# Cosine attention and a leaky-ReLU MLP on one core: where epsilon comes from, where transposes, scalings and key tiles stand in the order

## The chip, the cores and the metric

One core of one Trainium2 chip runs the whole program. The metric is the device time of one execution in microseconds. Five engines work side by side, each with its own instruction queue in program order: TensorE (PE, matrix multiplications; its weight loads are shown as PEld), VectorE (DVE), ScalarE (ACT), GpSimd (POOL) and SyncE (SP, which here only issues DMAs). They meet through semaphores.

## The reference

For 8 batches of 12 heads, 448 positions and 64 dimensions, `q` and `k` are divided by their norms plus an epsilon, and attention is taken with temperature `tau = 0.1`; its output, 3584 rows of 768, goes through a two-layer network with 2048 hidden units.

```python
q_n = q / (np.linalg.norm(q, axis=-1, keepdims=True) + 1e-06)
k_n = k / (np.linalg.norm(k, axis=-1, keepdims=True) + 1e-06)
scores = np.matmul(q_n, k_n.transpose(0, 1, 3, 2)) / tau
attn = np.exp(scores - np.max(scores, axis=-1, keepdims=True))
attn = attn / (np.sum(attn, axis=-1, keepdims=True) + 1e-09)
x = np.matmul(attn, v)            # then laid out as (3584, 768)
h = x @ w_in
out = np.maximum(0.01 * h, h) @ w_out
```

The scores of unit vectors are bounded, so the kernel subtracts no maximum.

## The kernel before

**Slots.** The 48 pairs of heads are 48 slots. For each slot the raw `q` and `k` are loaded (`load_qk`, on SP's queue, into 4 buffers), squared on POOL (`squares`, line 208 for slots 0 to 11, line 201 from slot 12 on), summed on DVE (`sums`, lines 222 and 216), turned into norms on ACT by a logarithm and an exponential (`roots`, lines 229 and 230), and divided on DVE (`normalise`: line 238 adds the epsilon, 239 takes the reciprocal, 255 or 245 multiplies and rounds to bf16, into `qn`). `hold` is a one-element POOL copy of `qn` (line 583): POOL's queue waits there until DVE has finished the multiplication, and the next squares stand behind it. `qn` is then transposed: for slots 0 to 11 by seven PE matmuls (line 269) and a DVE copy out of PSUM (line 310); for later slots by a DVE transpose (line 291), and for every second one of them by six SP DMAs (line 300) that gather two slots, a *unit*, into `qkT`.

**Scores, sums, values.** PE multiplies a tile of keys by all queries (line 331, or 402 in the third stage), ACT takes the exponential out of PSUM (lines 340 and 408). Row sums and values are further PE products of these tiles (line 351, or 427), the sums inverted on ACT by logarithm and exponential (362 and 363, or 436 and 439), and DVE multiplies the value products by them into `xT` (`scale`, line 382; `group_scale`, lines 452 and 458).

**The network.** `first` is one of 16 groups of hidden units for one chunk of columns (line 476, leaky ReLU on ACT at 485), `second` half of the output columns for 128 rows (line 507, DVE copy at 518, output DMA at 527). These groups have no hurry, and stand between pieces of attention.

**PSUM.** The 8 banks are dealt by `banks`, which takes the bank or pair of banks that was dealt longest ago. PE must wait where the work that last used a bank has not been read out of it.

**Stages.** All order is written by hand, with no scheduler behind it.

1. The loop over `s` from 0 to 5 (line 618) does the attention of batch 0, with filler matmuls (line 574) between. `j` counts pairs of slots whose values follow; `totals(j)` are their row sums, `products(j, e)` their values for even (`e = 0`) and odd dimensions, `scale(j, e)` the division. In an even `s` from 2 on, `totals(j)`, `products(j, 0)` and the transposes of slot `s + 1` follow each other on PE. `products(j, 1)` stands in the next, odd `s`, with both scalings: `scale(j, 0)` after its `normalise`, `scale(j, 1)` at its end.
2. A transition (lines 681 to 737), in which slots 6 to 10 are prepared between groups of the network of batch 0, and the key tiles of slots 6 and 7 in blocks.
3. `opened` (line 743), five steps for the rest of batch 1.
4. 42 *visits* (line 822). Each takes three key tiles of 32-column strips (`quad_tiles`), in `preps` visits prepares a slot, in `parts` visits makes the sums (`e = None`) or one half of the values (`e = 0`, `1`) of a group of heads, and is filled up with network groups by a planner that counts their columns. In a visit with a preparation, `normalise(s)` stands first, then `prepare` (transposes, load, `hold`, squares, and the sums of slot `s + 1`, in this order), then the first key tile, and behind it the group's products and scaling. Only where a group has a single member, does `prepare` stand behind the scaling (`alone`). `roots(s + 1)` stands near the visit's end, in front of its last network group, and so ahead of the next visit's exponentials in ACT's queue.
5. What is left of the network.

Of the kernel before, what the change touches and what calls it, by code (L numbers as in the profile page):

```python
# [8 lines left out]
F32 = mybir.dt.float32  # L9
BF16 = mybir.dt.bfloat16  # L10
AF = mybir.ActivationFunctionType
ALU = mybir.AluOpType
# [4 lines left out]
def kernel(  # L17
# [10 lines left out]
    nc = tc.nc  # L28
# [205 lines left out]
    def normalise(s):  # L234
        if s >= NSLOT:
            return
        r = smp.tile([128, 14], F32, name="r")
        nc.vector.tensor_scalar_add(ss[s], ss[s], 1e-6)  # L238
        nc.vector.reciprocal(r, ss[s])  # L239
        if s >= OLD:  # L240


            qn[s] = qnp.tile([128, 7, D, 2], BF16, name="qn")
            t, n = ("(m e)", "(e m)")[s % 2], 2
            nc.vector.tensor_tensor(  # L245
                qn[s].rearrange("p m d e -> p m e d"),
                raw[s].rearrange(f"p ({t[1:-1]} d) -> p m e d", e=n, d=D),
                r.rearrange(f"p {t} -> p m e", e=n).unsqueeze(3).to_broadcast([128, 7, 2, D]),
                op=ALU.mult,
            )  # L250
            return
        qn[s] = qnp.tile([128, 7, 2, D], BF16, name="qn")
        for x, lo, hi, r0 in ((raw[s][0], 0, 4, 0), (raw[s][1], 4, 7, 8)):
            nt = hi - lo
            nc.vector.tensor_tensor(
                qn[s][:, lo:hi],
                x.rearrange("p h t d -> p t h d"),
                r[:, r0 : r0 + 2 * nt].rearrange("p (h t) -> p t h", h=2)
                .unsqueeze(3).to_broadcast([128, nt, 2, D]),
                op=ALU.mult,  # L260
            )
# [55 lines left out]
    def scores(s, kis):  # L317
        key_tiles([(s, ki) for ki in kis])
# [49 lines left out]
    def products(j, e, po=None):  # L368
        b, jj = divmod(j, NQ)
        if po is None:  # L370
            po = banks(1, (j, e))
        pos[j, e] = po
        vm = vb[j].rearrange("p h t (d e) -> p h t e d", e=2)
        vr = vrb[b % 2].rearrange("p j g (d e) -> p j g e d", e=2)
        strip_products(j, po, lambda g, ki: vm[:, g, ki, e], lambda g: vr[:, jj, g, e])
# [177 lines left out]
    load_qk(3)  # L553
    tiny = cpool.tile([128, 1], F32, name="tiny")
    nc.vector.memset(tiny, 1e-18)
    warm = pep.tile([128, 2 * S], BF16, name="pe")[:, 0:512]
    nc.vector.memset(warm, 1.0)
    ones = cpool.tile([128, 32], BF16, name="ones")
# [56 lines left out]
    roots(1)  # L615


    for s in range(NPAIR):
        j = s // 2 - 1 if s >= 2 else None
        even = s % 2 == 0  # L620
        n = s + 2 if 0 < s < NPAIR - 2 else None
        last = s == NPAIR - 1
        if s == 1:
            roots(2)
        scores(s, (0,))
        if j is not None and not even:
            products(j, 1)
        scores(s, (1,))
        fill(2)
        if n:  # L630
            sums(n, (0,))
        if not last:
            normalise(s + 1)
            load_qk(s + 5)
        if j is not None and not even:
            scale(j, 0)
        if last:
            load_v(s // 2 + 1)
            load_v_rem(1)
            load_w_out(0)  # L640
        else:
            hold(qn[s + 1][:, 6, 0, 0:1])
        squares(s + 3)
        if s == 0:
            sums(2)
            load_v_rem(0, range(2, 4))
        if not even and not last:
            load_v(s // 2 + 1)
        if s != 1 and not last:
            load_w_in(max(s - 1, 0))  # L650
        if n:
            sums(n, (1,))
        scores(s, (2,))
        if not even or s == 0:
            fill(2)
        if n and not even:
            roots(n)
        if not even:
            scores(s, (3,))
        if j is not None and even:  # L660
            totals(j)
            products(j, 0)
        if not last:
            transposes(s + 1)
        if not even or s == 0:
            fill(2)
        if n and even:
            roots(n)
        if j is not None and not even:
            scale(j, 1)  # L670

    def attend(j):
        totals(j)
# [7 lines left out]
    deals["apart"] = False  # L681
    deals["width"] = 64
    s, j = NPAIR, NQ - 1
    totals(j)
    sums(s)
    po = banks(2)
# [19 lines left out]
    normalise(s + 1)  # L706
    load_qk(s + 5)
    sums(s + 2)
    scores(s, (0, 1))
    feed_groups(0, 1)  # L710
    transposes(s + 1)
    roots(s + 2)
    feed_groups(0, 1)
    scores(s, (2,))
    scores(s + 1, (0,))
    normalise(s + 2)
    hold(qn[s + 2][:, 6, 0, 0:1])
    squares(s + 4)
# [1 line left out]
    load_w_out(1)  # L720
    sums(s + 3)
    feed_groups(0, 2)
    transposes(s + 2)
    roots(s + 3)
    scores(s + 1, (1, 2))
    normalise(s + 3)
    load_qk(s + 6)
    sums(s + 4)
    feed_groups(0, 2)
    transposes(s + 3)  # L730
    roots(s + 4)
    scores(s + 1, (3,))
    normalise(s + 4)
    load_qk(s + 7)
    hold(qn[s + 4][:, 6, 0, 0:1])
    squares(s + 5)
    feed_groups(0, 3)

# [81 lines left out]
    for n, tiles in enumerate(visits):  # L822
        s = preps.get(n, NSLOT)
        g, e = parts.get(n, (None, None))
        alone = g is not None and e is not None and len(GROUPS[g]) == 1

        def prepare():
            if s < NSLOT:
# [4 lines left out]
                sums(s + 1)  # L833

        normalise(s)
        if not alone:
            prepare()
        quad_tiles(tiles[:1])
        if n == 0:
# [1 line left out]
        if g is not None:  # L841
# [2 lines left out]
                group_logs(g, po)  # L844
            else:
                group_scale(g, e, po)
        if alone:
            prepare()
        quad_tiles(tiles[1:])
        if g is not None and e is None:  # L850
# [73 lines left out]
```

## Time and profile before

| | us |
|---|---|
| median of 3 runs | 428.2 |
| lowest and highest | 426.79, 428.51 |
| the profiled execution | 426.59 |
| its span | 424.8 |

The span runs from the first to the last instruction that the profiler saw; 1.79 us of the profiled execution lie around it. PE is busy for 411.5 us of the span, ACT for 255.5, DVE for 221.6 and POOL for 114.8. The granted TensorE clock is full speed throughout. A row of the timeline has start, duration, engine, line, operation, tiles and shape; in brackets the time that the engine sat idle before it and what ended that. Several instructions of a kind are merged into one row (x16). "Slot 10" or "unit 1" below are names of this text for what the code counts so.

### The profile page before, as it was taken

The numbers are of one execution on the slowest core, as the hardware profiler recorded it, in microseconds if no ns is written. First come the engines' busy times: TensorE is split into PE (matmuls) and PEld (weight loads), VectorE is DVE, ScalarE is ACT, GpSimd is POOL, SyncE is SP. The second block draws the span as 40 slices with busy tenths as digits, with TensorE's granted clock in tenths as the row PEclk, the third lists the DMA queues.
The fourth block names the chain that finished last, engine by engine and source line by source line (L and its number), as shares of the span: only waits on it lengthen the run. The fifth ranks groups of instructions, "written<-read, shape, count | busy, mean of one in ns | idle before, by whom it ended". The sixth has DMA issues, their size and how long they took to land.

```text
span 424.8 us, 11331 instructions
## 1 busy us (share of the span) xinstructions
PE 411.5 (97%) x4779; PEld 213.6 (50%) x4797; DVE 221.6 (52%) x382; ACT 255.5 (60%) x430; POOL 114.8 (27%) x149
## 2 busy tenths in 40 slices
PE   7889999989999999999999999999999999999996
PEld 3334555434455555554455555554445555554563
DVE  5966877775578554776474874376412312120021
ACT  3886885668857686748875767647674454104300
POOL 3867353533234132413231432023010000000000
PEclk9999999999999999999999999999999999999999
DMA  6899999875375963575375583544441100010021
GB/s 170 163 236 226 215 239 175 195 208 144 56 201 156 214 156 58 158 175 144 78 162 146 116 231 91 115 125 125 83 88 39 77 38 3 36 76 0 2 74 74
DMA packets 41906, 53.82 MB, mean 127 GB/s; under 512 B 12544, under 2 KB 32256, under 8 KB 41856
## 3 DMA queue, kind: packets, MB, share of 16 engines
q1 hardware_dynamic: 25536, 40.85, 34.0%
q0 software_dynamic: 15488, 11.80, 19.4%
q8 instruction: 37, 0.61, 0.6%
q10 hardware_dynamic: 832, 0.46, 0.4%
q14 instruction: 13, 0.11, 0.1%
HBM read 45.61 MB, written 11.01 MB: 133 GB/s over the span
## 4 chain that ended last, share of the span: by engine, by line
PE 82%; DVE 8%; ACT 4%; DMA 3%; issue 2%; SPq 0%; POOL 0%; ACTq 0%; POOLq 0%; DVEq 0%
PE ps L476 32%; PE ps L507 31%; PE ps L427 8%; PE ps L402 6%; DMA qk_h<-in_k_dram 2%; PE ps L351 2%; PE ps L331 2%; DVE ss L216 1%; DVE qn L245 1%; DMA qk_h<-in_q_dram 1%; ACT pe L340 1%; ACT pe L408 1%; PE ps L269 1%; DVE ss L238 1%; DVE xT L382 1%
## 5 line engine op out<-in xcount | busy, mean ns | idle before, releaser
L507 PE MATMUL ps<-w_out_sb,hT 128*128 128x384 bf16 x896 | 151.4, 326 | 0.2 <-DVE xT L382 0.2
L476 PE MATMUL ps<-xT,w_in_sb 128*128 128x384 bf16 (+1 forms) x753 | 149.7, 352 | 0.9 <-issue 0.2
L408 ACT ACTIVATE pe<-ps 128x896 bf16<-128x896 f32 x126 | 109.1, 916 | 47.1 <-PE ps L402 43.2
L507 PEld LDWEIGHTS <-hT 128*128 128x128 bf16 x896 | 85.3, 98 | 64.7 <-issue 10.4
L476 PEld LDWEIGHTS <-w_in_sb 128*128 128x128 bf16 x768 | 73.1, 98 | 73.7 <-issue 8.4
L485 ACT ACTIVATE hT<-ps 128x384 bf16<-128x384 f32 (+1 forms) x128 | 68.0, 548 | 63.0 <-PE ps L476 62.2
L518 DVE COPY osb<-ps 128x384 f32<-128x384 f32 (+1 forms) x56 | 30.8, 550 | 106.4 <-PE ps L507 100.7
L201 POOL TENSOR_TENSOR sq<-qk_h 128x896 f32<-128x896 f32 x36 | 60.5, 1680 | 3.1 <-DMA qk_h<-in_q_dram 2.1
L583 POOL CAST seen<-qn 128x1 f32<-128x1 bf16 x46 | 8.5, 185 | 179.8 <-DVE qn L245 167.3
L245 DVE TENSOR_TENSOR qn<-qk_h,r 128x896 bf16<-128x896 f32 x36 | 42.7, 1185 | 1.4 <-DVE r L239 0.2
L402 PE MATMUL ps<-qkT 64*32 64x448 bf16 x1008 | 39.1, 353 | 2.0 <-DVE xT L382 1.4
L340 ACT ACTIVATE pe<-ps 128x896 bf16<-128x896 f32 x42 | 36.0, 916 | 7.4 <-PE ps L331 7.3
L216 DVE TENSOR_REDUCE ss<-sq 128x14 f32<-128x896 f32 x36 | 37.5, 1041 | 2.6 <-POOL sq L201 2.6
L238 DVE TENSOR_SCALAR ss<-ss 128x14 f32<-128x14 f32 x48 | 11.0, 230 | 49.1 <-ACT ss L230 48.8
L291 DVE STREAM_TRANSPOSE tt<-qn 128x448 f32<-128x448 f32 x36 | 29.6, 824 | 1.2
L452 DVE TENSOR_TENSOR xT<-ps,rb 128x448 bf16<-128x448 f32 x32 | 18.3, 613 | 21.5 <-PE ps L427 21.4
L427 PE MATMUL ps<-pe,vq 64*32 64x448 bf16 x1008 | 27.3, 349 | 0.0
L402 PEld LDWEIGHTS <-qkT 64*32 64x32 bf16 x1008 | 14.2, 91 | 23.2 <-issue 18.6
L229 ACT ACTIVATE ss<-ss,tiny 128x14 f32<-128x14 f32 x48 | 14.6, 304 | 15.3 <-DVE ss L216 11.2
L208 POOL TENSOR_TENSOR sq<-qk_h 128x384 f32<-128x384 f32 (+1 forms) x21 | 19.5, 945 | 12.7 <-DMA qk_h<-in_k_dram 12.6
L427 PEld LDWEIGHTS <-vq 64*32 64x32 bf16 x1008 | 14.7, 92 | 7.8 <-issue 0.3
L331 PE MATMUL ps<-qkT 64*64 64x448 bf16 (+1 forms) x132 | 13.4, 361 | 4.1 <-DVE qkT L310 2.0
(51 smaller groups left out, 216.9 us busy)
## 6 DMA issues: line engine op xcount, KB each, us to landing
qk_h<-in_q_dram SPq DMA_DIRECT2D x36, 224.0 KB, 4.0
qk_h<-in_k_dram SPq DMA_DIRECT2D x36, 224.0 KB, 4.4
out_dram<-osb SPq DMA_DIRECT2D x20, 384.0 KB, 2.5
qkT<-tt SPq DMA_DIRECT2D x72, 56.0 KB, 2.3
qkT<-tt SPq DMA_DIRECT2D x36, 112.0 KB, 2.3
vq<-in_v_dram POOLq DMA_DIRECT2D x16, 224.0 KB, 4.9
w_in_sb<-in_moe_w_in_dram POOLq DMA_DIRECT2D x4, 768.0 KB, 10.4
w_out_sb<-in_moe_w_out_dram POOLq DMA_DIRECT2D x2, 1536.0 KB, 21.6
```

The costliest lines, as they stand in the source:

```text
L201: gp.tensor_tensor(sq, raw[s], raw[s], op=ALU.mult)
L216: nc.vector.tensor_reduce(ss[s], sqs[s].rearrange("p (t d) -> p t d", d=D), axis=AX.X, op=ALU.add)
L245: nc.vector.tensor_tensor(qn[s].rearrange("p m d e -> p m e d"), raw[s].rearrange(f"p ({t[1:-1]} d) -> p m e d", e=n, d=D), r.rearrange(f" ...
L291: nc.vector.transpose(out=to.rearrange(("p g (c m) -> p m g c", "p g (m c) -> p m g c")[which], m=7), in_=qn[s].bitcast(F32).rearrange("p ...
L340: nc.scalar.activation(out=dst, in_=sc[:, :, :S], func=AF.Exp, scale=inv_tau)
L402: nc.tensor.matmul(out=sc[32 * strip : 32 * strip + 32, a, :S], lhsT=x[rows, c0 : c0 + 32], rhs=x[rows, 0:S], start=True, stop=True,)
L408: nc.scalar.activation(out=pq[u, i], in_=sc[:, :, :S], func=AF.Exp, scale=inv_tau)
L427: nc.tensor.matmul(out=po[32 * strip : 32 * strip + 32, w, :S], lhsT=weights, rhs=pq[us[x if two else 0], i][rows, a, :], start=(i == 0), ...
L476: nc.tensor.matmul(out=pm[:, :n], lhsT=w_in_sb[:, kt, m * 128 : (m + 1) * 128], rhs=xT[c // 2][:, kt, c0 : c0 + n], start=(kt == 0), stop= ...
L485: nc.scalar.activation(out=hT[c][:, m, :n], in_=pm[:, :n], func=AF.Prelu, alpha=0.01)
L507: nc.tensor.matmul(out=po2[:, :HALF], lhsT=hT[c][:, m, ts * 128 : (ts + 1) * 128], rhs=w_out_sb[:, m, half * HALF : (half + 1) * HALF], st ...
L518: nc.vector.tensor_copy(out=o[:, half * HALF : half * HALF + cut], in_=po2[:, :cut])
```

## The change

Five edits of order and one of an operand; the same matmuls, exponentials and transfers are issued.

- `normalise` adds the epsilon as a second tensor, a tile `eps` of 128x14 filled once at the start, in place of a constant.
- In the loop over `s`, an even step's transposes of slot `s + 1` stand between the row sums and the value products.
- `scale(j, 1)` moves from the end of an odd step to the next step, behind its `normalise`; the last one moves ahead of the transition.
- In the transition, the key tiles of slots 6 and 7 stand in blocks of three, two and two instead of two, two, two and one, and the network groups between them are dealt out anew.
- In visits, the preparation goes behind the products and the scaling in every visit that makes values, and in visit 0, which does a pair of batch 1.

On DVE the change of the visits concerns visit 0 and ten others (8, 13, 14, 20, 21, 25, 26, 29, 34 and 35): there the pair of scalings, which stood behind the transpose and the sums, comes right behind `normalise`. The order on PE, ACT, POOL and SP is the same in all visits. From `opened` on, the PSUM banks are dealt in the same pattern under other numbers.

```diff
-        nc.vector.tensor_scalar_add(ss[s], ss[s], 1e-6)
+        nc.vector.tensor_tensor(ss[s], ss[s], eps, op=ALU.add)
...
+    eps = cpool.tile([128, 14], F32, name="eps")
+    nc.vector.memset(eps, 1e-6)
...
+    late = []
     for s in range(NPAIR):
...
         if not last:
             normalise(s + 1)
             load_qk(s + 5)
+        if late:
+            scale(late.pop(), 1)
         if j is not None and not even:
             scale(j, 0)
...
         if j is not None and even:
             totals(j)
-            products(j, 0)
         if not last:
             transposes(s + 1)
+        if j is not None and even:
+            products(j, 0)
...
         if j is not None and not even:
-            scale(j, 1)
+            late.append(j)
...
     s, j = NPAIR, NQ - 1
+    scale(late.pop(), 1)
     totals(j)
...
     sums(s + 2)
-    scores(s, (0, 1))
+    feed_groups(0, 1)
+    scores(s, (0, 1, 2))
     feed_groups(0, 1)
     transposes(s + 1)
     roots(s + 2)
-    feed_groups(0, 1)
-    scores(s, (2,))
-    scores(s + 1, (0,))
     normalise(s + 2)
...
     sums(s + 3)
     feed_groups(0, 2)
+    scores(s + 1, (0, 1))
+    feed_groups(0, 1)
     transposes(s + 2)
     roots(s + 3)
-    scores(s + 1, (1, 2))
     normalise(s + 3)
     load_qk(s + 6)
     sums(s + 4)
     feed_groups(0, 2)
+    scores(s + 1, (2, 3))
+    feed_groups(0, 1)
     transposes(s + 3)
     roots(s + 4)
-    scores(s + 1, (3,))
...
-    feed_groups(0, 3)
+    feed_groups(0, 1)
...
-        alone = g is not None and e is not None and len(GROUPS[g]) == 1
+        scaling = n == 0 or e is not None
...
         normalise(s)
-        if not alone:
+        if not scaling:
             prepare()
         quad_tiles(tiles[:1])
         if n == 0:
             attend(NEWQ - 1)
...
-        if alone:
+        if scaling:
             prepare()
         quad_tiles(tiles[1:])
```

## The prediction

> **What bounds the kernel now.** I read the page first, then busy time by stretches of 10 us, then who waits for whom on PE, and then the timeline at each place that the change touches.
>
> ```profile
> span 424.8 us, 11331 instructions
> PE 411.5 (97%) x4779; PEld 213.6 (50%) x4797; DVE 221.6 (52%) x382; ACT 255.5 (60%) x430; POOL 114.8 (27%) x149
> PE 82%; DVE 8%; ACT 4%; DMA 3%; issue 2%; SPq 0%; POOL 0%; ACTq 0%; POOLq 0%; DVEq 0%
> 20.00:30.00 10.00, 8.57 (x103) 3.62 (x107) 7.83 (x17) 8.83 (x15) 5.82 (x9) 1.00 1.16 229
> 40.00:50.00 10.00, 10.00 (x89) 5.62 (x87) 9.48 (x22) 8.77 (x19) 2.61 (x4) 1.00 1.32 207
> PE ps L331 <- DVE qkT L310: 2.0, 4, 0.7
> PE ps L402 <- DVE xT L382: 1.4, 2, 1.3
> PE ps L402 <- DVE xT L452: 0.5, 3, 0.2
> ```
>
> PE sets the end: it has 82% of the chain that ended last and is idle for 424.8 - 411.5 = 13.3 us. The change issues the same matmuls, so it can gain only such idle time, or lose by adding to it. In the rows of stretches (after the length stand PE, PEld, DVE, ACT, POOL, the clock, DMA's busy share and GB/s) PE is idle for 1.4 us at 20 to 30, inside the loop over `s`, and for nothing at 40 to 50, in the transition. The three waits (us, times, longest) are those that the change is aimed at: scores behind the copy of the transposes, and key tiles behind a scaling that has not yet emptied their banks. A matmul's modelled end lies behind its turn, so true stalls are longer than these waits; I take them from starts.
>
> **The change part by part.** *Transposes ahead of the value products, and the later second scaling.*
>
> ```profile
> 21.02 0.74 PE L351 MATMUL ps<-pe,v_b 128*32 128x448 bf16 x12
> 21.88 0.56 PE L269 MATMUL ps<-id,qn 128*128 128x128 bf16 x7
> 22.48 0.62 DVE L310 COPY qkT<-ps 128x896 bf16<-128x896 bf16 x1 [1.32 <-PE ps L269]
> 23.16 0.36 PE L331 MATMUL ps<-qkT 64*128 64x448 bf16 x2 [0.72 <-DVE qkT L310]
> 24.09 1.16 DVE L255 TENSOR_TENSOR qn<-qk_h,r 128x512 bf16<-128x512 f32 x2
> 27.11 1.82 POOL L208 TENSOR_TENSOR sq<-qk_h 128x512 f32<-128x512 f32 x2 [1.54 <-DMA qk_h<-in_k_dram]
> 28.49 1.47 DVE L255 TENSOR_TENSOR qn<-qk_h,r 128x512 bf16<-128x512 f32 x2
> 32.17 0.36 PE L331 MATMUL ps<-qkT 64*128 64x448 bf16 x2 [0.72 <-DVE qkT L310]
> ```
>
> At `s = 2` products and transposes take PE from 21.02 to 21.88 + 0.56 = 22.44 in either order. With the transposes first they end near 21.7, DVE (idle for 1.32) copies until 22.3 under the products, and the scores start at 22.5 in place of 23.16: -0.6. At `s = 4` the same swap is worth at most the wait of 0.72; the norms must be there first. The late scaling lets them start 0.6 earlier, but then L255 runs into POOL's squares: at 28.49 it took 1.47 beside them, against 1.16 without them at 24.09, so I count only that it ends no later than before, at 28.49 + 1.47 = 29.96. The transposes' turn was 32.17 - 0.72 - 0.56 = 30.89, and 0.6 earlier is 30.3, so the norms are there: -0.6 again. The bank that the late scaling keeps is wanted next by `products(j, 1)` of step 5, after 32.17 - 0.6, and the scaling is over by 29.96 + 0.62. Sum -1.2; ends 0 (ACT takes the place of the wait) and -1.44 (both waits in full).
>
> *Larger blocks of key tiles.* PE had nothing to gain here by the row of 40 to 50. What the order shifts is ACT's queue:
>
> ```profile
> 51.59 1.82 POOL L208 TENSOR_TENSOR sq<-qk_h 128x512 f32<-128x512 f32 x2 [3.67 <-DMA qk_h<-in_k_dram]
> 54.04 0.31 ACT L229 ACTIVATE ss<-ss,tiny 128x14 f32<-128x14 f32 x1 [2.13 <-DVE ss L222]
> 54.18 1.16 POOL L113 DMA_DIRECT2D w_out_sb<-in_moe_w_out_dram  x1
> 54.63 0.72 DVE L238 TENSOR_SCALAR ss<-ss 128x14 f32<-128x14 f32 x1
> 36.48 1.19 POOL L113 DMA_DIRECT2D w_out_sb<-in_moe_w_out_dram  x1
> DMA to landing us min/median/max: 18.8/21.6/24.4
> 62.53 2.77 PE L507 MATMUL ps<-w_out_sb,hT 128*128 128x384 bf16 x16
> ```
>
> Slot 10's load lands at 51.59 and will not land sooner for what happens on PE; ACT stood 2.13 us before its norms, with an exponential behind it. The change puts the last two key tiles of slot 7 ahead of these norms, so that a PE that is 1.2 us early isn't stopped there. Slot 8's norms, on the other hand, now stand behind one exponential and one leaky ReLU more, and may reach their transposes late. The output weights are the next bound: if the longer of their two landings is the first half's, it lands at 36.48 + 24.4 = 60.9, and its first use, at 62.53, can move by 1.6, which is enough. Late next are slot 10's norms, whose `normalise` stands on DVE ahead of a scaling that empties two banks. On both slots together I put +0.25; the ends are 0 and +1.2 (all that the loop gained).
>
> *Epsilon from a tile.*
>
> ```profile
> L238 DVE TENSOR_SCALAR ss<-ss x48: 160/175/1462, 7.9 to 307.8; 128x14 f32<-128x14 f32 x48
> 83.44 1.46 DVE L238 TENSOR_SCALAR ss<-ss 128x14 f32<-128x14 f32 x1 [0.62 <-ACT ss L230]
> 83.19 1.68 POOL L201 TENSOR_TENSOR sq<-qk_h 128x896 f32<-128x896 f32 x1 [2.14 <-DMA qk_h<-in_q_dram]
> 84.93 0.24 DVE L239 RECIPROCAL r<-ss 128x14 f32<-128x14 f32 x1
> ```
>
> The addition of two small tensors is not in the trace: between the median 0.175 of L238 and the 0.24 of the reciprocal on the same shape, at most 48 x 0.065 = 3 us of DVE, hidden under DVE's idle 48%; I take 0. Two of its long cases show what it waits for: the one at 54.63 ends at 55.35 with POOL's issue of a load (54.18 + 1.16), the one at 83.44 ends at 84.90 with POOL's squares. The Trainium skill ("SBUF — State Buffer", Who interferes with whom) says that a one-source DVE instruction in a two-port mode shuts out all GpSimd work, and one with two SBUF inputs only GpSimd's reads. By it the first case goes (55.35 - 54.63 - 0.17 = 0.55 for slot 10, which would take the +0.25 away and make the sum -3.65) and the second stays, so that the edit would help only beside DMA issues. The sum below does not use it. If the second goes too, the multiplication behind it still meets the same squares, as at 28.49. The fill of the tile stands at the start and costs nothing.
>
> *Visit 0.*
>
> ```profile
> 84.57 2.77 PE L507 MATMUL ps<-w_out_sb,hT 128*128 128x384 bf16 x16
> 85.21 1.17 DVE L245 TENSOR_TENSOR qn<-qk_h,r 128x896 bf16<-128x896 f32 x1
> 87.11 3.73 SPq L300 DMA_DIRECT2D qkT<-tt  x6
> 87.94 1.14 DVE L382 TENSOR_TENSOR xT<-ps,rb 128x448 bf16<-128x448 f32 x2
> 89.13 0.76 PE L402 MATMUL ps<-qkT 64*32 64x448 bf16 x23 [0.18 <-DVE xT L382]
> 95.11 0.76 PE L402 MATMUL ps<-qkT 64*32 64x448 bf16 x24
> ```
>
> PE is through at 84.57 + 2.77 = 87.34 and really begins at 89.13: 1.8 lost, because the scaling (87.94) stands behind transpose and sums. Behind L245 it runs from 86.4 to 87.55; the second bank is free 0.2 late. That is -1.6. In return the transpose goes back by 1.14 and with it six DMAs, 3.73 us of SP's queue, and all that stands behind them there; they are issued by 92.0 and must land, and unit 1 is first read two visits on, in the row of 95.11, which would now come at 93.5: +0.5, between 0 and 1. ACT's norms wait for sums that come 1.14 later, and the exponentials behind them start at 89.5 or so, as before (89.1 + 0.4). Visit 0: -1.1; ends 0 and -2.
>
> *The other ten visits.*
>
> ```profile
> 132.41 0.38 PE L402 MATMUL ps<-qkT 64*32 64x448 bf16 x8
> 132.61 1.51 PE L427 MATMUL ps<-pe,vq 64*32 64x448 bf16 x56
> 136.53 1.14 DVE L452 TENSOR_TENSOR xT<-ps,rb 128x448 bf16<-128x448 f32 x2
> 136.65 0.31 ACT L229 ACTIVATE ss<-ss,tiny 128x14 f32<-128x14 f32 x1 [0.55 <-DVE ss L216]
> 137.20 0.35 PE L402 MATMUL ps<-qkT 64*32 64x448 bf16 x1
> 137.75 1.68 PE L427 MATMUL ps<-pe,vq 64*32 64x448 bf16 x56
> 244.45 1.06 PE L402 MATMUL ps<-qkT 64*32 64x448 bf16 x24
> ```
>
> Undisturbed, the products follow the first tile by 0.20 (132.41 to 132.61); where the tile waits for the scaling, by 0.55: 0.35 lost, at three places by the row of waits, and 0.30 at 244.45 (1.06 against 0.76 at 95.11). All four are behind changed visits: -1.35. Elsewhere the scaling was already early enough. Moved back by 1.14 are the transpose and the sums, and where the transpose completes a unit its six DMAs on SP, with loads and outputs behind them; those have three visits of time. POOL's `hold` and squares start from L245 as before. DVE's scaling now waits for PE's products with transpose and sums behind it, then L229 on ACT, and behind that the next exponentials: in the example L229 goes from 136.65 to 137.8 and the exponentials may start about 138.4, near where the late tile (137.75, with its own 0.35) let them start before. I take nothing for it; ends of the part 0 and -1.35, a loss apart (below).
>
> **Sum:** -1.2 + 0.25 - 1.1 - 1.35 = -3.4 us. Against the profiled execution's own 426.59 that is 423.2; it lay 1.6 under the median 428.2, against which the sum gives 424.8.
>
> **The rivals.** *The loads decide in the first 65 us.* DMA's busy share is above 1 in both stretches, and the loads of slot 10 and of the output weights don't come earlier. Then the loop's 1.2 is waited off in the transition, and 1.1 and 1.35 remain: 428.2 - 2.45 = 425.75. Against it: the weights leave 1.6, and slot 10's norms no longer stand ahead of the key tiles.
>
> *Slower: the delayed sums hold up the exponentials.* In eleven visits L216 goes back by 1.14, L229 with it, and ACT's queue is in order. At 136.65 ACT already waited 0.55 for L216. If all of it reached PE through banks that aren't emptied, 11 x 1.14 = 12.5 us; from 3.4/12.5 = 27% on it eats the gain, and from (3.4 + 2.14)/12.5 = 44% on the kernel is over 0.5% slower; at 60% it gives 428.2 - 3.4 + 7.5 = 432.3. Against it: ACT is busy 60%, and had to wait for PE at these places.
>
> *No effect:* PE's waits come back elsewhere (the wait for unit 1, or the next bank): 428.
>
> **Chances.** The forecast 0.60, the loads 0.17, slower 0.12, no effect 0.11. A measurement of this kernel tells about 0.5% from no change, that is under 426.06 or over 430.3: faster 0.66 (nearly all of the first case and half of the second, which lies 0.3 from the bound), same 0.22, slower 0.12. The likeliest case's own range is 423.0 to 426.2; with the loads' case and no effect it becomes 422.8 to 427.8.
>
> **What would show it.** Loop: L331 no longer waits for L310 in steps 3 and 5, and the first L476 starts 1.2 before 38.24. Transition: no idle PE up to the first L507, which starts near 61.6. Visit 0: L382 right behind L245, the wait of 1.26 gone, perhaps a wait for the six DMAs two visits on. Others: no wait of L402 for L452, L216 about 1.14 behind, L408 no later. It goes wrong if L408 waits for L229, if PE waits for transposes or weights between 50 and 65, or if the small addition with two inputs is long beside the squares.

## The result, and the profile after

The changed kernel takes 422.28 us (median of 4 runs, 422.09 to 422.94) against 427.64 us before (426.79 to 428.51, 4 runs): a ratio of 0.9877 [0.9851, 0.9904], 5.4 us less. Forecast were 424.8 us in a range of 422.8 to 427.8: the direction is right, the gain was larger than the range allowed. The two profiled executions differ by less, 426.59 - 422.44 = 4.15 us, with spans of 424.8 and 420.7.

The page of the changed kernel, its busy times and its chain:

```profile
span 420.7 us, 11326 instructions
PE 410.2 (98%) x4779; PEld 212.5 (51%) x4797; DVE 223.2 (53%) x383; ACT 254.7 (61%) x430; POOL 115.2 (27%) x149
PE 92%; DMA 4%; DVE 2%; issue 1%; POOL 0%; SPq 0%; ACT 0%; POOLq 0%; DVEq 0%
```

PE now has 92% of the chain, and DVE fell from 8% to 2%. What replaced DVE in small is DMA. PE's waits in the changed kernel (us, times, longest) name it:

```profile
PE ps L351 <- DMA v_b<-in_v_dram: 1.3, 1, 1.3
PE ps L331 <- DVE qkT L310: 0.6, 2, 0.3
```

The two waits of L402 for a scaling are gone, the wait for the copied transposes fell from 2.0 to 0.6, and PE waits 1.3 us for values, which it never did before. To see what each stage was worth, I compare the starts of the same PE work. The timeline of PE before:

```profile
35.86 0.75 PE L351 MATMUL ps<-pe,ones 128*32 128x448 bf16 x12
36.62 0.74 PE L351 MATMUL ps<-pe,v_b 128*32 128x448 bf16 x12
38.24 3.10 PE L476 MATMUL ps<-xT,w_in_sb 128*128 128x384 bf16 x18
251.08 0.38 PE L402 MATMUL ps<-qkT 64*32 64x448 bf16 x8
```

and after:

```profile
34.51 0.75 PE L351 MATMUL ps<-pe,ones 128*32 128x448 bf16 x12
36.76 0.75 PE L351 MATMUL ps<-pe,v_b 128*32 128x448 bf16 x12 [1.30 <-DMA v_b<-in_v_dram]
38.38 3.10 PE L476 MATMUL ps<-xT,w_in_sb 128*128 128x384 bf16 x18
61.95 2.77 PE L507 MATMUL ps<-w_out_sb,hT 128*128 128x384 bf16 x16
84.26 2.77 PE L507 MATMUL ps<-w_out_sb,hT 128*128 128x384 bf16 x16
93.05 0.76 PE L402 MATMUL ps<-qkT 64*32 64x448 bf16 x24
246.96 0.38 PE L402 MATMUL ps<-qkT 64*32 64x448 bf16 x8
```

| stage, up to | before | after | the stage alone | forecast |
|---|---|---|---|---|
| loop, first L476 | 38.24 | 38.38 | +0.14 | -1.2 |
| transition, first L507 | 62.53 | 61.95 | -0.72 | +0.25 |
| `opened`, L507 ahead of visit 1 | 84.57 | 84.26 | +0.27 | 0 |
| visit 0's scaling, L402 of visit 2 | 95.11 | 93.05 | -1.75 | -1.1 |
| the other ten, L402 behind the last | 251.08 | 246.96 | -2.06 | -1.35 |

The sum is -4.12, as by the spans (4.1); forecast was -3.4. None of the terms was met in size, and two have the wrong sign. The experiments ask why the loop gave nothing, whether the visits' gain stands alone, and why the medians lie a further 1.2 us apart.

### The profile page after: what moved, and what is told of

Its sections match the earlier page's. It is cut to its first block, busy times and chain, and to the rows that moved or that the text cites. A ratio compares the mean times of both kernels' runs of the same rounds, so it can differ in the third digit from the quotient of the medians.

```text
span 420.7 us, 11326 instructions
## 1 busy us (share of the span) xinstructions
PE 410.2 (98%) x4779; PEld 212.5 (51%) x4797; DVE 223.2 (53%) x383; ACT 254.7 (61%) x430; POOL 115.2 (27%) x149
## 4 chain that ended last, share of the span: by engine, by line
PE 92%; DMA 4%; DVE 2%; issue 1%; POOL 0%; SPq 0%; ACT 0%; POOLq 0%; DVEq 0%
PE ps L507 35%; PE ps L476 35%; PE ps L427 9%; PE ps L402 7%; PE ps L351 2%; DMA qk_h<-in_k_dram 2%; PE ps L576 2%; DMA v_b<-in_v_dram 2%; PE ps L331 1%; PE ps L269 1%; DVE qn L255 1%; POOL sq L208 0%; DVE ss L222 0%; DVE ss L238 0%; DVE osb L518 0%
## 5 line engine op out<-in xcount | busy, mean ns | idle before, releaser
L507 PE MATMUL ps<-w_out_sb,hT 128*128 128x384 bf16 x896 | 151.5, 327 | 0.2 <-DVE xT L382 0.2
L476 PE MATMUL ps<-xT,w_in_sb 128*128 128x384 bf16 (+1 forms) x753 | 149.8, 353 | 0.9 <-issue 0.2
L408 ACT ACTIVATE pe<-ps 128x896 bf16<-128x896 f32 x126 | 108.9, 916 | 41.6 <-PE ps L402 41.6
L507 PEld LDWEIGHTS <-hT 128*128 128x128 bf16 x896 | 85.3, 98 | 64.7 <-issue 10.4
L476 PEld LDWEIGHTS <-w_in_sb 128*128 128x128 bf16 x768 | 73.0, 98 | 73.5 <-issue 8.4
L245 DVE TENSOR_TENSOR qn<-qk_h,r 128x896 bf16<-128x896 f32 x36 | 42.5, 1181 | 1.2
L216 DVE TENSOR_REDUCE ss<-sq 128x14 f32<-128x896 f32 x36 | 37.5, 1041 | 2.5 <-POOL sq L201 2.5
L402 PE MATMUL ps<-qkT 64*32 64x448 bf16 x1008 | 37.0, 353 | 0.0
L238 DVE TENSOR_TENSOR ss<-ss,eps 128x14 f32<-128x14 f32 x48 | 11.0, 228 | 46.8 <-ACT ss L230 46.4
L229 ACT ACTIVATE ss<-ss,tiny 128x14 f32<-128x14 f32 x48 | 14.7, 306 | 19.1 <-DVE ss L216 16.7
L402 PEld LDWEIGHTS <-qkT 64*32 64x32 bf16 x1008 | 13.3, 91 | 20.0 <-issue 15.4
L576 PE MATMUL ps<-pe 128*128 128x512 bf16 x50 | 16.5, 454 | 1.6 <-DVE pe L559 1.5
```

The source lines that it names most:

```text
L216: nc.vector.tensor_reduce(ss[s], sqs[s].rearrange("p (t d) -> p t d", d=D), axis=AX.X, op=ALU.add)
L245: nc.vector.tensor_tensor(qn[s].rearrange("p m d e -> p m e d"), raw[s].rearrange(f"p ({t[1:-1]} d) -> p m e d", e=n, d=D), r.rearrange(f" ...
L402: nc.tensor.matmul(out=sc[32 * strip : 32 * strip + 32, a, :S], lhsT=x[rows, c0 : c0 + 32], rhs=x[rows, 0:S], start=True, stop=True,)
L408: nc.scalar.activation(out=pq[u, i], in_=sc[:, :, :S], func=AF.Exp, scale=inv_tau)
L476: nc.tensor.matmul(out=pm[:, :n], lhsT=w_in_sb[:, kt, m * 128 : (m + 1) * 128], rhs=xT[c // 2][:, kt, c0 : c0 + n], start=(kt == 0), stop= ...
L507: nc.tensor.matmul(out=po2[:, :HALF], lhsT=hT[c][:, m, ts * 128 : (ts + 1) * 128], rhs=w_out_sb[:, m, half * HALF : (half + 1) * HALF], st ...
```

## Experiments

Each kernel is compared with the kernel before, run beside it on the same chip; the three sets of its runs have medians of 427.58 to 427.67.

### Visit 0 alone

The kernel before, with `prepare` behind the scaling in visit 0 too.

```diff
-        alone = g is not None and e is not None and len(GROUPS[g]) == 1
+        alone = n == 0 or (g is not None and e is not None and len(GROUPS[g]) == 1)
```

> The kernel before, with the preparation behind the scaling in visit 0 alone. Theory of the places (the gain is the sum of the stalls that the two traces show at each place): PE's start of the first L476 group of visit 1 comes 1.75 us earlier, the rest of the order is untouched, so 1.75 us faster, ratio 0.996. Theory of the prediction: 1.1 us faster, with a wait of PE for the six DMAs of unit 1 in visit 2. Rival (sums delayed on ACT): no gain or a loss.

Measured: 426.04 us, a ratio of 0.9959 [0.9944, 0.9974], which is -1.75 us (-2.4 to -1.1). The timeline of PE in this kernel:

```profile
87.00 2.77 PE L507 MATMUL ps<-w_out_sb,hT 128*128 128x384 bf16 x16
89.71 0.76 PE L402 MATMUL ps<-qkT 64*32 64x448 bf16 x24
95.69 0.76 PE L402 MATMUL ps<-qkT 64*32 64x448 bf16 x24
```

From the network group to the tiles of visit 2 it takes 95.69 - 87.00 = 8.69 us, against 95.11 - 84.57 = 10.54 before: -1.85. The group is followed by its tiles after the 2.7 us that it lasts, and nothing is late two visits on.

### The other visits alone

The kernel before, with `prepare` behind the scaling in every visit that makes values, and visit 0 as it was.

```diff
-        alone = g is not None and e is not None and len(GROUPS[g]) == 1
+        alone = e is not None
```

> The kernel before, with the preparation behind the scaling in the ten other visits that make values. Theory of the places: four stalls of 0.53, 0.53, 0.53 and 0.30 and nothing else, so 2.0 us faster, ratio 0.9953. Prediction: 1.35 us faster. Rival (sums delayed on ACT): no gain or a loss.

Measured: 425.91 us, a ratio of 0.9947 [0.9927, 0.9968], which is -2.3 us (-3.1 to -1.4). The row of visit 0 among PE's waits stays, and the stall of visit 9 is gone. PE's waits in this kernel:

```profile
PE ps L402 <- DVE xT L382: 1.4, 2, 1.2
```

and its timeline at visit 9:

```profile
139.96 0.38 PE L402 MATMUL ps<-qkT 64*32 64x448 bf16 x8
...
141.97 2.29 PE L507 MATMUL ps<-w_out_sb,hT 128*128 128x384 bf16 x13
```

From the tile to the next network group it takes 141.97 - 139.96 = 2.01 us, as in the undisturbed visit in front of it. The kernel before took 2.54 for the same stretch, from the tile at 137.20 to this row of its timeline:

```profile
139.74 2.77 PE L507 MATMUL ps<-w_out_sb,hT 128*128 128x384 bf16 x16
```

The late scaling cost 0.53 there, not 0.35.

### The loop alone, and the change without it

The first kernel is the one before with the transposes ahead of the products and the late second scaling; the second is the changed kernel without these two.

```diff
+    late = []
...
+        if late:
+            scale(late.pop(), 1)
...
-            products(j, 0)
...
+        if j is not None and even:
+            products(j, 0)
...
-            scale(j, 1)
+            late.append(j)
...
+    scale(late.pop(), 1)
```

> The kernel before, with the transposes ahead of the value products and the later second scaling. Theory of the places: the row sums of j = 2 start 1.3 us earlier, then PE waits about as long for the values of j = 2, whose load is issued about 1 us later; 0 us in the end, ratio 1.000. Prediction: 1.2 us faster, 0.997. Rival: the load's delay is larger than the gain, up to 0.3 us slower.

> The changed kernel with the loop over slots as it was (products ahead of transposes, both scalings of a slot together); the epsilon tile, the transition and all visits are those of the change. Theory (the 1.2 us won in the loop are all given back to the load of the values of pass j=2, so the loop's edit is worth nothing here): 422.2 to 423.2 us, no separate wait of PE for v_b over 0.3 us, the first matmul of line L476 within 0.3 us of 38.3 on the axis of this trace. Rival (the prediction's sum: the loop gives 1.2 us that last): 423.5 to 424.2 us. Second rival (the loop's edit costs time, since the squares it slows make the next load late): below 422.0 us.

Measured: the loop alone 427.36 us, 0.9996 [0.9982, 1.0009]; the change without it 422.73 us, 0.9893 [0.9874, 0.9912], against 422.68, 0.9885 [0.9867, 0.9903], for the whole change in another set of runs. The first is a change of -0.8 to +0.4 us and leaves no room for 1.2. The second reaches from 422.2 to 423.8 and by itself says less. The traces say where it went. The loop alone makes PE wait, as the change does:

```profile
PE ps L351 <- DMA v_b<-in_v_dram: 1.5, 1, 1.5
```

Without the loop the first L476 starts at 37.75, 0.5 before what was expected and 0.6 before the changed kernel's 38.38, and the first L507 at 61.32 in place of 61.95. So in these two profiles the loop's edit even looks like a loss, which the medians don't confirm. It is worth nothing that these runs can measure.

### Early values

The changed kernel, with the loads of values of passes 1 and 2 issued on POOL ahead of the squares of their step.

```diff
+        if s == 3:
+            load_v(2)
         squares(s + 3)
...
-        if not even and not last:
-            load_v(s // 2 + 1)
+        if s == 1:
+            load_v(1)
```

> The changed kernel with the values of j = 2 loaded ahead of the squares in step 3 of the loop instead of behind them (POOL sits there waiting for a load). Theory of the places: PE's wait of 1.3 us for these values goes, the first network group starts 1.2 us earlier than 38.38, and what is left of the gain at the first L507 is 0.3 to 1.2 us, because the norms of the transition are late next: 421.2 to 422.0. Rival (the loads as a whole decide, whatever their order): the squares of slot 6 or 7 wait longer for their load by as much, and the time stays at 422.3.

> The changed kernel with the loads of the values of passes j=1 and j=2 issued ahead of the squares of their step, once more, beside the kernels of this call. If the 0.7 us that it won over the changed kernel come from the wait for v_b that is gone: 421.6 to 422.4 us, the first matmul of L476 near 37.1. If they were chance: 422.3 to 423.3 us.

Measured: 421.97 us beside 422.68 for the changed kernel, ratios 0.9875 [0.9861, 0.9888] and 0.9885 [0.9867, 0.9903]; the second time 422.37 (421.42 to 424.46), 0.9889 [0.9866, 0.9912]. The wait is gone. The timeline of the first profile:

```profile
36.83 0.36 PE L351 MATMUL ps<-pe,v_rem 128*32 128x448 bf16 x4
37.12 1.15 PE L476 MATMUL ps<-xT,w_in_sb 128*128 128x384 bf16 x6
...
52.75 0.34 PE L269 MATMUL ps<-id,qn 128*128 128x128 bf16 x3 [0.31 <-DVE qn L255]
...
61.25 0.44 PEld L507 LDWEIGHTS <-hT 128*128 128x128 bf16 x4 [0.42 <-DMA w_out_sb<-in_moe_w_out_dram]
61.25 0.66 PE L507 MATMUL ps<-w_out_sb,hT 128*128 128x384 bf16 x3
```

The first L476 starts 1.26 earlier than in the changed kernel, which is the loop's gain. The first L507 starts only 0.70 earlier: most of the rest goes at slot 9's transposes, which now come before their norms (52.05 to the next L476 at 52.93 is 0.88, against 53.28 to 53.69, 0.41, in the changed kernel). Without that PE would have stood at L507, since the weight load in front of it waits until 61.25 for the output weights. In the second profile the first L476 starts at 36.63, PE waits 0.57 at slot 6's transposes, and the first L507 starts at 61.16: again little is left of the gain. The medians of the first set lie 0.7 us apart, but their intervals overlap, and the second median is only 0.3 below the changed kernel's. A faster kernel than the changed one was not shown.

### Later weights

The kernel of the early values, with the third load of the first layer's weights one step later, next to the fourth; and the kernel before with this alone.

```diff
-        if s != 1 and not last:
-            load_w_in(max(s - 1, 0))
+        for i in {0: (0,), 2: (1,), 4: (2, 3)}.get(s, ()):
+            load_w_in(i)
```

> The kernel of the early values, with the third load of the feed-forward weights (index 2) issued one step later, together with the fourth. Theory (the loads of this stage stand in one another's way, and what is left of the loop's gain hangs on them): 421.0 to 421.9 us, the executions within 0.6 us of each other. Rival (with the wait for v_b gone nothing in the loop waits for a load any more): 421.6 to 422.4 us, as the early values alone. Against both: over 422.6 us, where the late weights then hold up the norms of slots 7 and 8.

> The kernel before with nothing changed but the third load of the feed-forward weights issued one step later, together with the fourth. Theory (the kernel before loses 0 to 2 us in the transition, from execution to execution, where the load of slot 7 lands late and the norms of slots 7 and 8 follow late; that load shares the DMA engines with these weights): 426.3 to 427.0 us with a spread under 1 us, and no wait of PE line L269 for DVE line L255 over 0.5 us. Rival (the spread has another cause): 427.2 to 428.0 us, with a spread of 2 us as before.

Measured: with the early values 425.1 us (421.8 to 428.98), 0.9945 [0.9913, 0.9977], about 2.7 us worse than without. A loss had been allowed for, but by late norms of slots 7 and 8; those cost PE a wait of 0.52 at slot 7, and the larger wait stands elsewhere. The timeline of PE:

```profile
61.09 0.76 PE L331 MATMUL ps<-qkT 64*64 64x448 bf16 x12
64.94 2.77 PE L507 MATMUL ps<-w_out_sb,hT 128*128 128x384 bf16 x16 [3.09 <-DMA w_out_sb<-in_moe_w_out_dram]
```

The output weights stand behind these loads on POOL's queue. They were issued at 39.61 and landed 25.3 us later; in the kernel of the early values they were issued at 36.16 and took 25.0, in the changed kernel 37.39 and 23.5, before 36.48 and 24.4. In the three that is a landing at 60.9 to 61.2, in this one at 64.9. It is a floor under the first 62 us: what the loop wins beyond it would be waited off. The profiled execution took 425.16 us; the five slowest of the twelve, 427.15 to 428.98, have no trace, and their mean granted clock is 0.991 to 0.995, against 0.998 here. So part of this kernel's loss may go with the clock, of which the last section speaks, though two runs at 0.995 and 0.996 took only 423.53 and 422.81.

The kernel before with the later weights has 426.81 us, 0.9998 [0.9978, 1.0019]. Eight of its twelve runs lie between 426.38 and 426.89, as the theory wanted, but four between 428.2 and 430.3. In its profile, one of the eight, PE waits for L255 nowhere in the transition for over 0.5 us; the 1.2 us among its waits stand at 9.24, at the very first transposes, where the kernel before waits 0.79. So these weights are not the whole cause of the spread of before, and what moves slot 7's load from one execution to the next stays open.

### The transition alone

The kernel before with the transition's new blocks: three, two and two key tiles in place of two, two, two and one, and the network groups dealt as in the change.

```diff
-    scores(s, (0, 1))
     feed_groups(0, 1)
+    scores(s, (0, 1, 2))
+    feed_groups(0, 1)
     transposes(s + 1)
     roots(s + 2)
-    feed_groups(0, 1)
-    scores(s, (2,))
-    scores(s + 1, (0,))
     normalise(s + 2)
...
```

> The kernel before, with the larger blocks of key tiles in the transition alone. Theory of the places: 0.3 to 0.45 us faster by the profile. Theory of the scatter: the runs of before lie in two clusters, 426.6 to 427.1 and 428.2 to 428.5, because the load of slot 10 lands now sooner, now later, and an exponential stands behind its norms; then this edit takes the slow cluster away, all its runs lie within 0.8 us of each other, and the median is 1 to 1.5 us faster than that of before. If the scatter stays, its cause is elsewhere.

Measured: 426.93 us (426.23 to 427.93), 0.9983 [0.997, 0.9995]: -0.7 us (-1.3 to -0.2), where the prediction had +0.25. The theory of the scatter failed: the runs span 1.7 us, not 0.8, and the gain is not 1 to 1.5. What else the new order may help against is in the profiles of other kernels with the old order. In that of "visit 0 alone", the transition's first transposes, those of slots 6 and 7:

```profile
41.74 0.40 PE L269 MATMUL ps<-id,qn 128*128 128x128 bf16 x4 [0.20 <-DVE qn L255]
42.84 0.34 PE L269 MATMUL ps<-id,qn 128*128 128x128 bf16 x3 [0.70 <-DVE qn L255]
46.41 0.81 PE L269 MATMUL ps<-id,qn 128*128 128x128 bf16 x7 [0.33 <-DVE qn L255]
```

Slot 7's load had landed late there, and POOL's squares with it:

```profile
33.06 1.82 POOL L208 TENSOR_TENSOR sq<-qk_h 128x512 f32<-128x512 f32 x2 [1.88 <-DMA qk_h<-in_k_dram]
```

All that stands behind it on POOL's queue came later too, and the squares of slot 8 met DVE's multiplication for slot 6. POOL and DVE in this kernel:

```profile
40.07 2.29 POOL L208 TENSOR_TENSOR sq<-qk_h 128x512 f32<-128x512 f32 x2
40.35 2.43 DVE L255 TENSOR_TENSOR qn<-qk_h,r 128x512 bf16<-128x512 f32 x2
```

L255 took 2.43 us there, against 1.16 in the first profile of the kernel before, and the transposes wait for it. In the traces of all kernels there are nine blocks of transposes between 38 and 56 that such a wait of 0.3 us or more cuts in two, and in front of each L255 took 2.2 to 2.5 us beside squares.

Below is the time from the first L476 to the first L507 in one profiled execution of each kernel (the one whose output weights were 3.09 us late is left out).

| order of the transition | us from first L476 to first L507 |
|---|---|
| old | 24.29 (before), 24.73 (later weights), 25.34 (loop alone), 25.36 (epsilon alone), 26.25 (visit 0 alone), 26.31 (others alone) |
| new | 23.55 and 23.57 (the change, twice), 23.57 (without the loop), 24.08 (without the tile), 24.13 and 24.53 (early values, twice), 24.93 (transition alone) |

The medians are 25.35 and 24.08. The new order stands slot 7's transposes 4.1 us behind slot 6's (45.43 - 41.32) in place of 3.0 (44.17 - 41.18). In five of the six traces with the old order slot 7's are stretched to 0.81 us or split by a wait, and the sixth is the profile of before; in the seven with the new order they don't wait. But the trace that is left out of the table has the new order too, and there they wait 0.52, and slot 6's transposes wait in two of the seven (0.70 with the transition alone, 0.57 with the early values). So the new order helps at slot 7 and does not end the sensitivity.

The execution on which the prediction's sum was made has the shortest transition of the old ones, 1.06 below their median. How much of that a usual execution loses is not shown: the other five profiled executions lie 0.1 to 1.4 us above the medians of their own kernels, and the transition alone gains 0.7 by the medians, not 0.7 and another 1.06.

### The epsilon tile alone, and the change without it

```diff
-        nc.vector.tensor_scalar_add(ss[s], ss[s], 1e-6)
+        nc.vector.tensor_tensor(ss[s], ss[s], eps, op=ALU.add)
```

The first kernel is the one before with this and its tile; the second is the changed kernel with the constant again. The third is the changed kernel once more, run beside them.

> The kernel before with the epsilon from a tile alone. Theory of the ports: L238's case of 0.72 beside POOL's issue of the output weights goes to 0.17, those beside POOL's squares stay; no PE wait hangs on it: 427.5, ratio 0.999 to 1.000. Rival: 0.4 us or more faster.

> The changed kernel with the constant in place of the tile. Theory of the ports: only the addition beside the issue of the output weights (0.55 us near 55) waits again, and PE isn't waiting for it: within 0.2 us of the changed kernel, 422.3. Rival (the eps tile carries the 0.4 us that the other parts leave, by less waiting of DVE): 422.7 or more, with L238 long beside POOL's DMA issues at several places.

> The changed kernel itself, a second time. Theory of the loads (a load of slot 7 lands now in time, now 1 to 2 us late, and shifts POOL's queue and the norms behind it): its runs scatter over 2 us as those of before do, 422 to 424.5, and its profile may show waits of the transposes for the norms between 40 and 50. Theory that the change removed the scatter: all runs within 1 us, 422.0 to 423.0.

Measured: the tile alone 427.7 us, 1.0002 [0.9988, 1.0016]; the change without it 423.45 us, 0.9907 [0.9889, 0.9926]; the changed kernel 422.68 us (421.5 to 423.29), 0.9885 [0.9867, 0.9903]. The changed kernel's runs span 1.8 us, so the change did not remove the scatter, as one of the theories had it. One execution without the tile took 1078.45 us, for which no cause was found; the others took 422.74 to 424.55. The groups of line 238 with the tile alone:

```profile
L238 DVE TENSOR_TENSOR ss<-ss,eps x48: 158/174/1491, 8.0 to 309.3; 128x14 f32<-128x14 f32 x48
```

The median is 0.174 us, as with the constant (0.175). The median without the tile lies in the rival's range, 0.77 us above the changed kernel's. The rival's sign is not in the trace: L238 is long there once between 15 and 85 us, for 1.00 at 52.70 beside squares, and never beside a DMA issue. The intervals overlap, so whether the 0.77 are more than scatter stays open. The profiled execution, the slowest of the four ordinary ones, loses 1.4 us at half clock, which the last section shows.

## Why the prediction was right or wrong

Of the 2.5 us between the forecast of 424.8 and the 422.28 measured, 0.56 are the base: the median of the kernel before was 428.2 when the forecast was made and 427.64 with one run more. The other 2.0 are the gain, -5.4 in place of -3.4. By the parts run alone, the loop gave 1.0 less than forecast and the transition 0.95 more. That these two errors cancel is luck; what is left are the visits, -4.05 in place of -2.45, the two terms that were sized too small.

**The loop's swap and late scaling (-1.2 forecast, +0.14 measured): the mechanism was right, its size too, and the gain did not last.** The forecast put the scores of step 3 at 22.5 and gave 0.6 to each of two steps. The timeline of the changed kernel:

```profile
22.49 0.36 PE L331 MATMUL ps<-qkT 64*128 64x448 bf16 x2
30.83 0.36 PE L331 MATMUL ps<-qkT 64*128 64x448 bf16 x2
```

That is 0.67 and, with step 5, 1.34 earlier; the row sums of pass 2 came 1.35 earlier. The step that failed is that the loop's end was taken to move with PE. The values of pass 2 are loaded by POOL behind the squares of slot 6, and the same edit had moved DVE's multiplication onto them. The timeline of the changed kernel there:

```profile
27.25 2.00 DVE L255 TENSOR_TENSOR qn<-qk_h,r 128x512 bf16<-128x512 f32 x2
27.42 2.52 POOL L208 TENSOR_TENSOR sq<-qk_h 128x512 f32<-128x512 f32 x2 [2.42 <-DMA qk_h<-in_k_dram]
29.89 0.81 POOL L162 DMA_DIRECT2D v_b<-in_v_dram  x1
```

Before, the squares ran from 27.11 for 1.82 us and the load was issued at 28.88. It now goes out 1.01 later, 0.70 of it for the longer squares and 0.31 because they start later, behind their own load. It lands 6.8 us after its issue, 6.6 before, and PE wants it 1.35 earlier. I had noted the squares beside L255, and counted what they do to L255, not what L255 does to them and to POOL's queue behind. The rival "the loads decide in the first 65 us" named the right thing, a gain waited off at a load, but not this load; with the early values 0.56 of 1.26 is lost again further on, and the output weights stand ready to take more.

**Transition (+0.25 forecast, -0.72 between the profiles, -0.7 [-1.3, -0.2] alone).** The step that failed is the sentence that PE had nothing to gain here by the row of 40 to 50. PE was 10.00 busy of 10.00 in it, and still held stalls, since a matmul's modelled end fills them. By starts, the five blocks of L269 take 2.32 us before (41.57 - 41.18 and so on) and 1.99 after, where each is followed by a network group: 0.33 less. The key tiles of L331 in the same stretch give the rest, 0.4 us. Neither slot 10's norms nor slot 8's came late.

The base has its own flaw: the profiled execution's time was 1.6 below the median of its runs, and adding the sum to that median took for granted that the difference lay outside the change's reach. The short transition of this profile says that some of it may lie inside. The runs don't settle it, since the transition alone gains no more by its medians than between the two profiles.

**`opened` (0 forecast, +0.27).** It was not costed. One key tile waits for an output copy; PE's timeline in the changed kernel:

```profile
74.42 0.38 PE L331 MATMUL ps<-qkT 64*64 64x448 bf16 x3 [0.24 <-DVE osb L518]
```

The block of twelve and its successor take 74.95 - 73.42 = 1.53, against 75.26 - 74.01 = 1.25 before. The kernels with the loop, the tile, visit 0 or the other visits alone have the same wait of 0.2 among PE's waits, though their banks are dealt as before, and this stage takes 22.30 to 22.33 us in them, 22.31 in the changed kernel and 22.04 in the profile of before. So the 0.27 are not the change's: the profile of before is the short one here too. What sets it was not looked into.

**Visit 0 (-1.1 forecast, -1.75 measured, and -1.75 alone).** The gain of 1.6 was nearly right. The term that failed is the +0.5 for six DMAs that go late. DVE's and SP's timeline in the changed kernel, and how long those six took to land:

```profile
85.88 1.14 DVE L382 TENSOR_TENSOR xT<-ps,rb 128x448 bf16<-128x448 f32 x2
...
87.64 3.72 SPq L300 DMA_DIRECT2D qkT<-tt  x6
```

```profile
DMA to landing us min/median/max: 1.9/2.0/2.6
```

The scaling stands right behind L245, as forecast. The last of the six begins about 0.6 before 87.64 + 3.72 = 91.36 and lands 1.9 to 2.6 later, between 92.7 and 93.4; the tiles two visits on begin at 93.05 and don't wait. It was just in time. I had no landing of such a DMA in the sum, and took the middle of a range where a row of the trace would have put it near its lower end. That it fits by so little is luck.

**The other ten visits (-1.35 forecast, -2.06 measured, -2.3 [-3.1, -1.4] alone).** The mechanism was right at the places forecast: by starts, 0.60 up to the tiles behind visit 9 (142.45 to 139.79, against -2.06 before), then 0.53, 0.53 and 0.30. The mis-sized term is 0.35 per stall. It came from the 0.55 between the first tile's start at 137.20 and that of the products, less the usual 0.20, and left out that the two tiles behind the products are late as well: from the first of them to the network group it takes 0.65 (139.09 to 139.74), where it takes 0.50 undisturbed (133.93 to 134.43). Three stalls by 0.53 and one of 0.30 are 1.89, and small drifts make the rest.

**The slower rival** did not come, though what it names was there. ACT in the changed kernel's visit 1:

```profile
88.58 0.31 ACT L229 ACTIVATE ss<-ss,tiny 128x14 f32<-128x14 f32 x1 [2.03 <-DVE ss L216]
89.03 2.51 ACT L408 ACTIVATE pe<-ps 128x896 bf16<-128x896 f32 x3
```

ACT waits 2.03 us for the delayed sums, and over the visits the waits of L229 for L216 grew from 11.2 to 16.7 us. But the exponentials start at 89.03, before the 89.5 allowed for, and among PE's waits there is none for L408: the wait fits into time in which ACT had nothing to do.

**Epsilon (0 forecast, 0 measured).** The rule that the sum did not use is borne out at the two places that the prediction named. DVE in the changed kernel:

```profile
55.34 0.18 DVE L238 TENSOR_TENSOR ss<-ss,eps 128x14 f32<-128x14 f32 x1
...
83.13 1.39 DVE L238 TENSOR_TENSOR ss<-ss,eps 128x14 f32<-128x14 f32 x1 [0.62 <-ACT ss L230]
```

and POOL beside it:

```profile
54.90 1.17 POOL L113 DMA_DIRECT2D w_out_sb<-in_moe_w_out_dram  x1
...
82.80 1.68 POOL L201 TENSOR_TENSOR sq<-qk_h 128x896 f32<-128x896 f32 x1 [2.17 <-DMA qk_h<-in_q_dram]
```

At 55.34 POOL issues the load of the output weights, and the addition takes 0.18 where the constant took 0.72 beside the same issue. At 83.13 POOL's squares run, and it takes 1.39, about as before (1.46). Other traces repeat it: beside the issue of these weights between 54 and 57 us the constant took 0.71 or 0.72 in six traces, the tile 0.17 or 0.18 in five. Beside this issue the edit helps, beside squares not, as the Trainium skill ("SBUF — State Buffer", Who interferes with whom) has it for a DVE instruction with two SBUF inputs. It is no rule for every issue: the constant took 0.17 beside an issue of the first layer's weights (loop alone, at 23.01), and the tile 0.90 beside issues of values (later weights, at 37.97); neither was looked into. No time followed from the edit, since slot 10's norms were not late.

**The sum of the parts.** By their ratios, the parts alone give -1.75 - 2.3 - 0.7 - 0.2 + 0.1 = -4.9 us, and the whole -4.9 and -5.3 in its two sets of runs: the parts add up within their intervals, and nothing large is hidden between them. Why the medians differ by 0.8 to 1.2 us more than the first two profiles stays open; the short transition and `opened` in the profile of before (1.06 and 0.27) are where to look.

## What to carry to other kernels

A stretch in which an engine is fully busy by its rows can still hold stalls, and a stall's price is the time from one start to the next piece's start, held against the same pair of starts undisturbed (2.54 against 2.02 us); parts of it read from modelled ends came out a third too small. Before a gain on the way to a load is counted, the landing of that load and of the next one are looked up, and whether the edit itself slows the queue that issues them. And where the profiled execution lies at an end of its runs, part of what the runs lose may be missing from the profile, so the sum should not be carried over to the median without asking which stage makes the difference. Here that stayed open, since one profile shows one execution.

## What the runs showed of the hardware

**DVE and POOL slow each other, and PE pays.** In the changed kernel L255 (two inputs from SBUF) took 2.00 us beside the squares, against 1.16 undisturbed, and the squares 2.52, against 1.82; before, with a shorter overlap, L255 took 1.47 and the squares stayed at 1.82. In the transition of visit 0 alone it was 2.43 beside squares of 2.29. What I had not expected is that PE pays in two ways: through transposes that wait for L255, and through a load that POOL issues behind the squares.

**After a short idle time PE's clock was halved.** In the changed kernel without the tile, PE stood 1.80 us before the values. The stretches of 1 us from the end of this wait on (behind the length stand PE, PEld, DVE, ACT, POOL, clock, DMA share, GB/s):

```profile
36.00:37.00 1.00, 0.13 (x4) 0.12 (x8) 0.00 (x0) 0.68 (x3) 1.00 (x2) 1.00 1.16 213
37.00:38.00 1.00, 1.00 (x16) 0.48 (x12) 0.00 (x0) 0.00 (x0) 0.93 (x2) 0.51 1.12 215
38.00:39.00 1.00, 1.00 (x20) 0.39 (x16) 0.43 (x1) 0.00 (x0) 0.98 (x2) 0.50 1.11 207
39.00:40.00 1.00, 1.00 (x13) 0.27 (x6) 0.20 (x2) 0.00 (x0) 1.00 (x2) 0.50 1.15 217
```

For 3 us the granted clock was half, and the twelve matmuls at 36.87 took 1.22 us in place of 0.75; the first L476 started 3.01 behind the first of them (39.88), against 1.62 in the changed kernel (38.38 - 36.76), so 1.4 us were lost. The changed kernel's second profile had a wait of 1.99 there, and that of the early values with later weights 3.09 at the first L507, both at full clock. The Trainium skill ("TensorE: Matmul & The Clock Gate", Part 1: The HAM clock gate) says that the clock halves after at least one idle window of about 3.4 us, and that the window runs freely. The 1.80 us are less than such a window, so the trace differs from the rule as stated; that it is hit or miss from one execution to the next would go with a free-running window, which these runs can't show. Here a wait of 1.8 us cost PE 1.4 us beyond itself, in one trace. The runs without a trace suggest that it was not the only time: this execution's mean granted clock is 0.996, and seven of the twelve runs with the later weights lie at 0.996 or below, as does one run each of the loop alone, the change without the loop and the second set of the early values, but none of the 68 runs of the kernel before beside the experiments (0.998 or more). What their clock followed, no trace shows.
